# Masking every fourth key block in one call, and issuing the value products a quarter of a block later

## The chip, the core and the metric

The kernel runs on one core of a Trainium2 chip. TensorE (PE) does the matmuls; VectorE (DVE), ScalarE (ACT) and GpSimd (POOL) do the elementwise work; SyncE (SP) issues all DMAs. The metric is the time of one execution on the device in microseconds: the median of three runs is 743.41 us (743.22 to 743.43).

## The reference

One transformer-like block on 2048 tokens of width 512, in float32. A gate mixes sliding-window attention (32 heads of 16 channels, each query sees the 256 keys up to its own) with an MLP that has a tanh GELU:

```python
scores = einsum("bhqd,bhkd->bhqk", q, k) * 16 ** -0.5
mask = (i - j >= 0) & (i - j < 256)
p = softmax(where(mask, scores, -1e9))
a = einsum("bhqk,bhkd->bhqd", p, v) -> (S, 512) @ wo
b = gelu(x @ w1 + b1) @ w2 + b2
g = sigmoid((x * gate_w).sum(-1))
out = g * a + (1 - g) * b
```

## The kernel before

**Two programs woven into one order.** The kernel writes the order of every engine by hand. A *dense* generator (`dense`) yields PE's large work: the projections `qkv`, the MLP (`mlp`, per chunk of 512 tokens and half of the hidden width an *up stage* of `u` tiles and a *down stage* of `y` tiles), and `final` (the output projection). Each step is a group of three matmuls (`mm3`, L109 to L111: high and low halves of the operands), and stands for 681 ns of the order's own clock. `tick` moves this clock on, and `after(ns, fn)` puts an engine's instruction into the program at a later time of it; `need(key)` brings forward what a step depends on. These numbers set only the order in which instructions are written. On the chip each engine takes its list in order and waits on semaphores.

**Attention** is cut into 8 groups of 4 heads and 16 blocks of 128 keys, so 128 units `u`. The main loop (`for u in range(-LEAD, NU)`) handles unit `u` and, 12 units ahead of it, the row maxima of block `m = u + LEAD`. It goes through four quarters `i`; `ORDER` is "m", "s", "p", "f":

- "m": `att_max` makes one tile `sm` of scores (L522, PSUM, at most 320 columns), and VectorE takes its masked row maximum (L527, a reduction and a short read of the accumulator into `M`). The four `sm` tiles of a block come in the order 1, 0, 3, 2 (`XOR`). I call them the first to the fourth.
- "s": `att_exp` makes a tile `st` of transposed scores of unit `u` (L567), with the maxima subtracted through four extra rows of `qs`; ScalarE takes its exponential into `pt` (L589), which holds both key halves (`hf`) and two head pairs of a block. Behind the last of them GpSimd sets to 0 what the window excludes: `sel`, with L583 for each half of the partitions (`r`) and each end of the window (`e`), the near end in columns 0 to 63, the far end in 256 to 319. Three blocks in four have one call of `sel` for both key halves (four selects of 64 x 256 elements); the fourth has one call for each key half (four selects of 64 x 128 each). The last 12 units (`late`) are masked on VectorE (L577).
- "p": at quarter `PVAT`, one unit late, `att_pvs(u - 1)` does the products of the exponentials with the values for a whole chunk of four blocks (L611, 72 or 96 short matmuls), if `u - 1` is the last block of its chunk. It needs the masks of all blocks that it reads, the chunk's own four and up to two ahead of them. There are 32 such calls, 29 of them at `PVAT`; the last three come elsewhere.
- "f": `fill` takes dense steps worth a quarter of `STEP`.

In the up stage a quarter is "m", "s", "p" and one dense step. In the other stages two quarters are joined: "m", "s", "p" of both, and then the dense steps of both.

**What ties them.** `sm` and `st` are PSUM tags of three buffers each, and a call of `att_pvs` takes one of each for its results:

```python
p = ps.tile([128, 320], F32, tag="sm", bufs=3, ...)                  # att_max
p = ps.tile([128, 320], F32, tag="st", bufs=3, ...)                  # att_exp
pv = [ps.tile([128, T], F32, tag=tag, bufs=3, ...) for tag in ("st", "sm")]  # att_pvs
```

A tile gets the buffer that was given back first. So the results of the products get the buffer of the tile three places back in the same tag, and PE waits until VectorE has taken its maximum, or ScalarE its exponential. They go out through ScalarE (L632) and VectorE (L635) into `nd`.

**Other work on the same engines.** Each `u` tile of the MLP passes through ScalarE and VectorE in six steps (`gelu`, L722 to L740). The weights are split into two halves on ScalarE and VectorE (L179, L183). After every fourth block `att_rows` turns the maxima into rows: three short operations on VectorE (L539, L540, L542) and eight copies on GpSimd (L549).

## Time and profile before

| what | before |
|---|---|
| median of three runs | 743.41 us |
| the profiled execution, its span | 745.76 us, 744.0 us |
| ScalarE busy | 57% of the span |
| DMA queue of SyncE | 179168 packets, 170.97 MB, 82.9% of 16 engines |
| chain that ended last | PE 86%, DVE 4%, DMA 4%, ACT 3%, issue 2% |
| PE clock granted | full in all 40 slices |

A row of the timeline gives the start and the duration in us, then engine, line and operation, what is written and read, the sizes, how many instructions are merged and, in brackets, how long the engine stood idle before and what ended that. A row of groups ends with busy time, the mean in ns, and the idle time before them with what ended it. A row of stretches gives the length and then the busy time of PE, weight loads, DVE, ACT and POOL, the granted clock, the share of DMA and GB/s. A matmul's duration contains its passage through the array, so matmuls that follow each other overlap.

### The profile page before, as it was taken

Reading aid. Unit: us, or ns where it says so; the run is one execution under the profiler, and the core shown is the slowest. Engines: PE = TensorE matmul, PEld = TensorE weight load, DVE = VectorE, ACT = ScalarE, POOL = GpSimd, SP = SyncE. Lnnn points to the kernel's source line nnn. Section 1 sums busy time; section 2 is a strip of 40 time slices with the busy share of each in tenths; the row PEclk is TensorE's granted clock in tenths of the full one; section 3 lists DMA queues with packets and bytes.
Section 4 is the critical chain, followed back from the end, with each engine's and each line's share of the span. In section 5 each row is a group of like instructions: output and inputs, shape, how many; then the busy total and the mean of one; then the engine's idle time right before and its main releaser. Section 6 shows DMA issues by size and latency. Waiting matters only on the chain.

```text
span 744.0 us, 17964 instructions
## 1 busy us (share of the span) xinstructions
PE 731.7 (98%) x6129; PEld 604.6 (81%) x6129; DVE 513.6 (69%) x1567; ACT 421.0 (57%) x972; POOL 356.9 (48%) x846
## 2 busy tenths in 40 slices
PE   9999999999999999999999999999999999999998
PEld 7888888887788888888887877888888888878776
DVE  3632325799768867886898789767867886784552
ACT  4434532359447845764695478447735853785450
POOL 4200000349655855776576557746765775620000
PEclk9999999999999999999999999999999999999999
DMA  9989798999994797799567888996799899567573
GB/s 306 351 269 407 262 390 273 267 317 222 262 250 120 176 253 203 172 225 273 148 160 181 223 211 227 252 249 157 178 265 241 177 240 244 137 206 216 175 259 111
DMA packets 179259, 172.12 MB, mean 231 GB/s; under 512 B 56672, under 2 KB 122976, under 8 KB 179168
## 3 DMA queue, kind: packets, MB, share of 16 engines
q1 hardware_dynamic: 179168, 170.97, 82.9%
q8 instruction: 49, 0.80, 0.5%
q14 instruction: 42, 0.34, 0.2%
HBM read 108.53 MB, written 62.39 MB: 230 GB/s over the span
## 4 chain that ended last, share of the span: by engine, by line
PE 86%; DVE 4%; DMA 4%; ACT 3%; issue 2%; SPq 1%; DVEq 0%; ACTq 0%
PE sm L522 9%; PE st L567 8%; PE pv_sm L611 7%; PE y L109 7%; PE y L110 7%; PE y L111 7%; PE u L109 6%; PE u L110 5%; PE u L111 5%; PE qk L109 4%; PE qk L111 4%; PE qk L110 4%; PE v L109 2%; PE v L111 2%; PE v L110 2%; PE pv_st L611 2%
## 5 line engine op out<-in xcount | busy, mean ns | idle before, releaser
L527 DVE CUSTOM_DVE_ANT_0 jm<-sm,mask 128x320 bf16<-128x320 f32 (+4 forms) x512 | 238.1, 465 | 95.6 <-PE sm L522 61.8
L589 ACT ACTIVATE pt<-st 128x320 f32<-128x320 f32 (+4 forms) x512 | 199.2, 424 | 136.5 <-PE st L567 134.5
L583 POOL TENSOR_SCALAR_AFFINE_SELECT pt<-pt 64x256 f32<-64x256 f32 (+1 forms) x538 | 215.3, 420 | 119.0 <-ACT pt L589 108.6
L522 PE MATMUL sm<-kd,qd 96*128 96x320 f32 (+4 forms) x512 | 153.3, 311 | 3.6 <-DVE M L527 3.0
L567 PE MATMUL st<-qs,ks 128*128 128x320 f32 (+4 forms) x512 | 153.8, 309 | 1.1 <-ACT pt L589 1.0
L549 POOL CAST qs<-tt 4x256 fp32r<-4x256 f32 x256 | 120.3, 470 | 55.1 <-DVE tt L542 44.6
L522 PEld LDWEIGHTS sm<-kd,qd 96*128 96x128 f32 x512 | 96.4, 188 | 28.4 <-DVE M L527 8.8
L567 PEld LDWEIGHTS st<-qs,ks 128*128 128x128 f32 x512 | 97.1, 190 | 18.0 <-ACT pt L589 2.4
L109 PE MATMUL y<-w,h 128*128 128x512 f32 x224 | 88.6, 396 | 0.6 <-DVE sqh L728 0.6
L110 PE MATMUL y<-w,h 128*128 128x512 f32 x224 | 88.0, 393 | 0.0
L111 PE MATMUL y<-w,h 128*128 128x512 f32 x224 | 87.9, 393 | 0.0
L109 PE MATMUL u<-mx,w 128*128 128x512 f32 x196 | 80.1, 409 | 0.4 <-DVE sqh L728 0.4
L110 PE MATMUL u<-mx,w 128*128 128x512 f32 x196 | 77.4, 395 | 0.0
L111 PE MATMUL u<-mx,w 128*128 128x512 f32 x196 | 77.1, 393 | 0.0
L611 PE MATMUL pv_sm<-pt,vbuf 64*32 64x320 f32 (+4 forms) x1408 | 73.0, 346 | 0.0
L611 PE MATMUL pv_st<-pt,vbuf 64*32 64x320 f32 (+4 forms) x1408 | 72.7, 346 | 0.0
L611 PEld LDWEIGHTS pv_sm<-pt,vbuf 64*32 64x32 f32 x1408 | 49.4, 106 | 20.2 <-issue 2.4
L326 DVE TENSOR_TENSOR qke<-qk,qke 128x512 fp32r<-128x512 f32 x32 | 22.0, 688 | 46.2 <-ACT qke L323 30.2
L323 ACT ACTIVATE qke<-qk 128x512 fp32r<-128x512 f32 x32 | 19.1, 598 | 56.5 <-PE qk L111 32.9
L111 PEld LDWEIGHTS y<-w,h 128*128 128x128 f32 x224 | 42.1, 188 | 9.8
L109 PEld LDWEIGHTS y<-w,h 128*128 128x128 f32 x224 | 42.4, 189 | 4.6 <-DVE sqh L728 0.8
L339 POOL MEMSET vx<- 128x32 f32 x16 | 2.4, 155 | 89.4 <-DMA SK<-qke 26.6
(148 smaller groups left out, 1329.8 us busy)
## 6 DMA issues: line engine op xcount, KB each, us to landing
kd<-SK SPq DMA_DIRECT2D x32, 384.0 KB
qs<-SQ SPq DMA_DIRECT2D x64, 192.0 KB
mx<-XT SPq DMA_DIRECT2D x24, 512.0 KB
SQ<-qke SPq DMA_DIRECT2D x16, 512.0 KB
SK<-qke SPq DMA_DIRECT2D x16, 512.0 KB
ND<-nd SPq DMA_DIRECT2D x32, 256.0 KB
raw_w<-in_B_w_dram SPq DMA_DIRECT2D x28, 256.0 KB
ks<-SK SPq DMA_DIRECT2D x32, 192.0 KB
```

The source lines that it names most:

```text
L109: nc.tensor.matmul(p, lh, rh, start=first, stop=False)
L110: nc.tensor.matmul(p, lh, rl, start=False, stop=False)
L111: nc.tensor.matmul(p, ll, rh, start=False, stop=last)
L323: nc.scalar.activation(e[:, h], p, AF.Copy)
L326: nc.vector.tensor_sub(e[:, 1 - h], p, f32(e[:, h]))
L522: nc.tensor.matmul(p[:, :w], qd[0:96, n, pr, 128 * j:128 * (j + 1)], kd[0:96, n, pr, k1 - w:k1], start=True, stop=True)
L527: nc.vector.tensor_tensor_reduce(junk[:, :w], p[:, :w], mask[:, 320 - w:320], 1.0, -3e38, ALU.add, ALU.max, M[:, 2 * (b % RB) + hb, pr:pr ...
L549: nc.gpsimd.tensor_copy(dst, src.unsqueeze(1).broadcast_to([4, 2, RB, 32]))
L567: nc.tensor.matmul(p[:, :w], ks[:, slot(g_, kb // NB), pr, at:at + 128], qs[:, pr, k0:k0 + w], start=True, stop=True)
L583: nc.gpsimd.affine_select(out=v, in_=v, pattern=[[0, v.shape[1]], [1 - 2 * e, 64]], compare_op=ALU.is_ge, fill=0.0, base=-e, channel_multi ...
L589: nc.scalar.activation(pt[:, hf, pr, :w], p[:, :w], AF.Exp, scale=SCALE)
L611: nc.tensor.matmul(pv[r // 64][32 * i:32 * i + 32, q - c * T:e - c * T], vts[g_, b // NB][r:r + 64, v:v + 32], rhs(r), start=start, stop=s ...
```

## The change

Two numbers change. `both` no longer leaves out the last block of a chunk, so all blocks that are masked on GpSimd have one call of `sel` for both key halves, behind the last exponential. `PVAT` is 3 in place of 2.

```diff
-        both = not late and kb % NB < NB - 1
+        both = not late
-PVAT = 2
+PVAT = 3
```

On PE, at the products of the last chunk of the first head group, in an up stage (`u_2` is a dense tile, `sm_12_k` and `st_0_k` are tiles k of block 12 and of block 0 of the next head group; `sm_12_1` and `sm_12_0`, the first two of block 12, stand ahead of these rows). Before:

```order
L109 MATMUL u_2_2810<-mx_2149,w_2_1418 128x512
L110 MATMUL u_2_2810<-mx_2149,w_2_1418 128x512
L111 MATMUL u_2_2810<-mx_2149,w_2_1418 128x512
L522 MATMUL sm_12_3_2862<-kd,qd 128x320
L567 MATMUL st_0_2_2865<-qs,ks 128x320
L611 MATMUL pv_3_sm<-pt_10_2471,vbuf 32x64
```

and now:

```order
L109 MATMUL u_2_2796<-mx_2145,w_2_1418 128x512
L110 MATMUL u_2_2796<-mx_2145,w_2_1418 128x512
L111 MATMUL u_2_2796<-mx_2145,w_2_1418 128x512
L522 MATMUL sm_12_3_2848<-kd,qd 128x320
L567 MATMUL st_0_2_2851<-qs,ks 128x320
L109 MATMUL u_2_2796<-mx_2145,w_2_1418 128x512
L110 MATMUL u_2_2796<-mx_2145,w_2_1418 128x512
L111 MATMUL u_2_2796<-mx_2145,w_2_1418 128x512
L522 MATMUL sm_12_2_2862<-kd,qd 128x320
L567 MATMUL st_0_3_2865<-qs,ks 128x320
L611 MATMUL pv_3_sm<-pt_10_2463,vbuf 32x64
```

A dense step, the fourth `sm` tile and the fourth `st` tile now stand ahead of the products. Three places back in `sm` was the first tile of the block (`sm_12_1`), and now is the second (`sm_12_0`). At 13 of the 29 calls five matmuls pass the products in this way; at the other 16, in a down stage, the pair alone does, as here (`sm` of block 4 of the last head group, `st` of block 8 of the one before it), before:

```order
L522 MATMUL sm_4_0_9076<-kd,qd 128x320
L567 MATMUL st_8_1_9080<-qs,ks 128x320
L109 MATMUL y_10_9022<-w_10_6421,h_10_8764 128x512
L110 MATMUL y_10_9022<-w_10_6421,h_10_8764 128x512
L111 MATMUL y_10_9022<-w_10_6421,h_10_8764 128x512
L522 MATMUL sm_4_3_9096<-kd,qd 128x320
L567 MATMUL st_8_2_9099<-qs,ks 128x320
L611 MATMUL pv_1_sm<-pt_2_8664,vbuf 32x64
```

and now:

```order
L522 MATMUL sm_4_0_8984<-kd,qd 128x320
L567 MATMUL st_8_1_8988<-qs,ks 128x320
L109 MATMUL y_10_8934<-w_10_6365,h_10_8674 128x512
L110 MATMUL y_10_8934<-w_10_6365,h_10_8674 128x512
L111 MATMUL y_10_8934<-w_10_6365,h_10_8674 128x512
L522 MATMUL sm_4_3_9004<-kd,qd 128x320
L567 MATMUL st_8_2_9007<-qs,ks 128x320
L522 MATMUL sm_4_2_9010<-kd,qd 128x320
L567 MATMUL st_8_3_9014<-qs,ks 128x320
L611 MATMUL pv_1_sm<-pt_2_8578,vbuf 32x64
```

On VectorE, at the first of these two places (`jm_12_k` is the maximum of `sm_12_k`, the row after it the read of the accumulator). Before:

```order
L527 ISA jm_12_1_2829,M_12_2826<-sm_12_1_2827,mask 128x320
L734 SCALAR_TENSOR_TENSOR x1h_0_2754_2762<-sqh_0_2754_2763,x1h_0_2754_2762 128x512
L728 SCALAR_TENSOR_TENSOR sqh_1_2809_2817<-u_1_2755,x1h_1_2809_2816 128x512
L539 TENSOR_SCALAR nm<-M_8_2565 128x8x2
L540 SCALAR_TENSOR_TENSOR nm<-M_8_2565,nm 128x8x2
L542 STREAM_TRANSPOSE tt<-nm 128x256
L527 ISA jm_12_0_2853,M_12_2826<-sm_12_0_2851,mask 128x320
L527 ISA jm_12_3_2864,M_12_2826<-sm_12_3_2862,mask 128x320
L740 TENSOR_TENSOR h_0_2754<-x1h_0_2754_2762,h_0_2754 128x512
L734 SCALAR_TENSOR_TENSOR x1h_1_2809_2816<-sqh_1_2809_2817,x1h_1_2809_2816 128x512
L635 TENSOR_TENSOR nd_3_2927<-nd_3_2927,pv_3_sm 128x512
L527 ISA jm_12_2_2935,M_12_2826<-sm_12_2_2933,mask 128x320
```

The rows down to the third maximum (`jm_12_3`) are the same now; the fourth, `jm_12_2`, has moved up to directly behind the first L740, ahead of L734 and L635. On GpSimd, around the products of the first chunk (`pt_k` is block k, `xN` the count of equal instructions), before:

```order
L583 AFFINE_SELECT pt_2_1910<-pt_2_1910 64x4x64 x4
L583 AFFINE_SELECT pt_3_1965<-pt_3_1965 64x2x64 x8
L549 CAST qs<-tt 4x2x4x32 x6
L583 AFFINE_SELECT pt_4_2016<-pt_4_2016 64x4x64 x4
L549 CAST qs<-tt 4x2x4x32 x2
```

and now:

```order
L583 AFFINE_SELECT pt_2_1910<-pt_2_1910 64x4x64 x4
L583 AFFINE_SELECT pt_3_1965<-pt_3_1965 64x4x64 x4
L549 CAST qs<-tt 4x2x4x32 x3
L583 AFFINE_SELECT pt_4_2012<-pt_4_2012 64x4x64 x4
L549 CAST qs<-tt 4x2x4x32 x5
```

Block 3 has four selects of twice the width in place of eight, and of the row copies between its masks and those of block 4 three instead of six are left. SyncE issues the same DMAs; the stores of `nd` and what hangs on them move by one or two places.

## The prediction, on record before the changed kernel ran

> **What bounds the kernel now.** I read the page first (busy time by engine), then the busy time by stretch, then who waited for whom on TensorE (PE), and last the timeline around the products of the values, which the change moves.

> ```profile
> PE 731.7 (98%) x6129; PEld 604.6 (81%) x6129; DVE 513.6 (69%) x1567; ACT 421.0 (57%) x972; POOL 356.9 (48%) x846
> 165.00:650.00 485.00, 479.88 (x4618) 398.26 (x4618) 380.39 (x1252) 305.33 (x709) 321.97 (x767) 1.00 0.85 210
> PE sm L522 <- DVE M L527: 3.0, 7, 0.8
> ```

> PE is busy for 731.7 of 744.0 us. In the stretch from 165 to 650 us, where 28 of the 32 calls of `att_pvs` stand (I call such a call a product group; the 29th and last that is moved starts at 650.5), it is busy for 479.88 of 485 us at the full clock. So PE's own work bounds the kernel, and a change gains only what PE waits (about 5 us in that stretch) and loses whatever wait it adds. The change adds no matmul and takes none away. GpSimd (POOL), whose work the change halves in part, is busy for less than half of the span, and in the list of PE's waits no GpSimd instruction stands for this stretch. The longest entry is the third row: PE waits for a row maximum of VectorE (DVE) before a matmul at L522, 3.0 us in 7 times. That kind of wait is the one to follow.

> **Masks.** Of the 128 blocks, 116 are masked on GpSimd, 29 of them in two calls before and in one now.

> ```profile
> L583 POOL TENSOR_SCALAR_AFFINE_SELECT pt<-pt 64x256 f32<-64x256 f32 x334 | 149.1, 467 | 89.7 <-ACT pt L589 84.2
> ...
> L583 POOL TENSOR_SCALAR_AFFINE_SELECT pt<-pt 64x128 f32<-64x128 f32 x204 | 66.1, 343 | 29.3 <-ACT pt L589 24.4
> ...
> L734 DVE SCALAR_TENSOR_TENSOR x1h<-sqh,x1h 128x512 f32<-128x512 f32 x56 | 41.9, 748 | 1.2 <-ACT sqh L731 1.2
> ...
> L728 DVE SCALAR_TENSOR_TENSOR sqh<-u,x1h 128x512 f32<-128x512 f32 x56 | 38.3, 684 | 2.8 <-ACT u L725 2.4
> ```

> The 204 short selects (66.1 us busy, 343 ns mean) become 102 of the long form, at 467 ns 47.6 us: GpSimd loses 18.5 us of work. None of it stands on PE's path, so I cost it at nothing; what hides it is GpSimd's idle time (119.0 us before these selects). The price is at the end of a block: after the last exponential four selects of 467 ns (1.87 us) must run where four of 343 ns (1.37 us) did, so the masks are ready 0.5 us later. The nearest place is this one:

> ```profile
> 327.91 1.27 POOL L583 TENSOR_SCALAR_AFFINE_SELECT pt<-pt 64x128 f32<-64x128 f32 x4 [1.23 <-ACT pt L589]
> ```

> The group that reads these masks starts at 328.90 and will be ready at 329.20 (next part). Its first matmuls need the selects at columns 0 to 64 of both row halves, the first and third of four: 327.91 + 3 x 0.467 = 329.31, a wait of 0.1 us; by all four at their mean 329.78, of 0.6. I take 0.1 and keep 0 to 0.6. At the other groups the last exponential ends at least half a microsecond earlier against the group.

> Two VectorE operations of one size differ by 64 ns, 748 for L734 with both operands in SBUF and 684 for L728 with one in PSUM, over 56 of them 3.6 us, while GpSimd runs beside them. If that loss goes with the count of GpSimd's instructions (102 fewer of 846, 12%), the change gives VectorE 0.4 us back in the whole kernel. [...]

> **Products a quarter later.** In the up stage the group is put behind one more group of three matmuls and one more pair of L522 and L567, in the down stage behind one more pair; the rows stand in the section on the change. The matmuls are the same ones, so their time is nothing by itself. What changes is which buffers the group gets. `sm` has three buffers; a group takes one, and starts only when VectorE has read the tile three places back. Before that is the first of the four `sm` tiles of the block in hand, now the second. For `st` and the exponentials likewise. VectorE does the four maxima in order, and the instructions ahead of the second maximum are the same before and now. So its end can be read from this trace and held against the time at which PE will be ready. In the up stage:

> ```profile
> 228.30 0.31 PE L567 MATMUL st<-qs,ks 128*128 128x320 f32 x1
> ...
> 229.29 0.31 PE L567 MATMUL st<-qs,ks 128*128 128x320 f32 x1
> 229.53 0.24 PE L611 MATMUL pv_sm<-pt,vbuf 64*32 64x64 f32 x1
> ```
> ```profile
> 230.36 0.45 DVE L527 CUSTOM_DVE_ANT_0 jm<-sm,mask 128x320 bf16<-128x320 f32 x1
> 230.75 0.08 DVE L527 DVE_READ_ACCUMULATOR2_ANT M<- 128x1 f32 x1
> ```

> A quarter lasts 229.29 - 228.30 = 0.99 us, so PE will be ready at 229.53 + 0.99 = 230.52. The second maximum, which stands behind the three operations of `att_rows`, ends at 230.83, and PE starts 0.05 us after such an end (379.85 + 0.08 to 379.98, below): a wait of **0.36**. Before, this buffer was wanted only after the group, whose 2 us hid the maximum. In the down stage:

> ```profile
> 599.02 0.31 PE L522 MATMUL sm<-kd,qd 96*128 96x320 f32 x1
> 599.17 0.32 PE L567 MATMUL st<-qs,ks 128*128 128x320 f32 x1
> 599.32 0.32 PE L522 MATMUL sm<-kd,qd 96*128 96x320 f32 x1
> ...
> 600.70 0.24 PE L611 MATMUL pv_sm<-pt,vbuf 64*32 64x64 f32 x1
> ```
> ```profile
> 600.86 0.48 DVE L527 CUSTOM_DVE_ANT_0 jm<-sm,mask 128x320 bf16<-128x320 f32 x1
> 601.27 0.08 DVE L527 DVE_READ_ACCUMULATOR2_ANT M<- 128x1 f32 x1
> ```

> A pair lasts 0.30 us, PE will be ready at 601.00, the maximum ends at 601.35: a wait of **0.40**. The group that waits already before:

> ```profile
> 378.76 0.35 PE L567 MATMUL st<-qs,ks 128*128 128x320 f32 x1
> 379.67 0.30 PE L611 MATMUL pv_st<-nil,vbuf 64*32 64x64 f32 x2 [0.55 <-ACT pt L589]
> 379.98 0.24 PE L611 MATMUL pv_sm<-nil,vbuf 64*32 64x64 f32 x1
> ```
> ```profile
> 379.85 0.08 DVE L527 DVE_READ_ACCUMULATOR2_ANT M<- 128x1 f32 x1
> ...
> 381.41 0.08 DVE L527 DVE_READ_ACCUMULATOR2_ANT M<- 128x1 f32 x1
> ```

> It waits 0.62 us for an exponential (379.67 against 379.05, 0.29 after the matmul before it) and 0.31 for the first maximum, 0.93 together. Now the fourth `sm` tile stands ahead, ready at 378.76 + 0.85 = 379.61 and started at 379.98 (0.37), and the group, ready 0.39 later at 380.37, starts after the second maximum at 381.54 (1.17): 1.54 in all, **0.61** more than before. Two others in the up stage:

> ```profile
> 178.92 0.24 PE L611 MATMUL pv_st<-nil,vbuf 64*32 64x64 f32 x1
> ...
> 180.40 0.08 DVE L527 DVE_READ_ACCUMULATOR2_ANT M<- 128x1 f32 x1
> ...
> 449.33 0.24 PE L611 MATMUL pv_st<-nil,vbuf 64*32 64x64 f32 x1
> ...
> 450.81 0.08 DVE L527 DVE_READ_ACCUMULATOR2_ANT M<- 128x1 f32 x1
> ```

> 178.92 + 0.99 = 179.91 against 180.53, **0.62**; 449.33 + 0.99 = 450.32 against 450.94, **0.62**. Three more groups (328.90, 430.69, 584.96) come close; each costs between nothing and the 0.36 above, and I take 0.1 each, 0.3. At the remaining 21 the second maximum ends before PE is ready.

> Part of this is paid back where VectorE's backlog makes PE wait soon afterwards anyway:

> ```profile
> 186.97 0.42 PE L522 MATMUL sm<-kd,qd 96*128 96x320 f32 x1 [0.79 <-DVE M L527]
> ...
> 464.05 0.41 PE L522 MATMUL sm<-kd,qd 96*128 96x320 f32 x1 [0.36 <-DVE M L527]
> ```

> The first of these follows the group at 178.92 by 8 us, the second ends a row of waits after 449.33. VectorE uses the time that PE stands, so I give back half of the one 0.62 and all of the other. After the groups at 229, 379 and 600 no such wait stands within 10 us, so nothing comes back.

> The sum: 0.36 + 0.40 + 0.61 + 0.62 + 0.62 + 0.3 + 0.1 (masks) = 3.0 us, less 0.3 and 0.6, and less 0.3 for what the new order takes off elsewhere (VectorE can do the fourth maximum while the group runs; an estimate between nothing and the 0.55 of the one exponential wait above): **1.8 us more**. On the queues of SyncE and GpSimd the stores of the group's result and the copies of the rows move with it; nothing on PE waits for these within a block, and I cost them at nothing, with half a microsecond either way. The profiled execution took 745.76 us with a span of 744.0; the median is 743.41. The sum is a difference, so it goes on the median: 743.41 + 1.8 = **745.2 us**.

> **The rivals.** *All is paid back.* VectorE's backlog is a debt that PE pays once, at the group or later; then only the three groups with no later wait count and half of these, and the time is 743.41 + 0.7 = 744.1. For it speaks that 3.0 us of PE's waits hang on the same maxima; against it that three of the five large terms have no wait behind them. *Not slower:* a lighter GpSimd lets VectorE go faster; it decides if the second maximum comes 0.4 to 0.6 us earlier at the five places. Then the added waits fall away and the old 0.93 and some 0.2 elsewhere go: 742.3. Against it stands that the count above gives 0.4 us in the whole kernel. [...] *The masks come last:* if selects wait behind the row copies or run at their mean, a third of the 21 groups that read the newest block's mask first lose some 0.3 us each, 2 us more than forecast: 747.2. Against it, the order on GpSimd keeps these selects ahead of the copies. *The change does not bite,* since the group was waiting for something else anyway: 743.4, against which stands that of PE's waits in this trace one alone, the 0.55 us at 379.67, is of a group for a buffer.

> **How the numbers follow.** About 0.2%, 1.5 us, is what a measurement of this kernel can tell from no change, so slower begins at 744.9. Chances: the forecast 0.52, paid back 0.24 (with no bite), not slower 0.13, masks 0.11. Of the forecast four fifths lie above 744.9, with the masks 0.53 slower; the not-slower case reaches below 741.9 in a third, 0.04 faster; the rest 0.43 is within. The range from 742.8 to 747.0 leaves out the ends of the last two cases.

> **What will show it.** In the changed kernel's waits of PE, L611 behind M of L527 should appear with some 2.5 to 3.5 us, at groups near 180, 231, 381, 451 and 601 us, and the exponential wait at 379 should be gone. L583 should be 436 instructions of one kind, GpSimd some 18 us less busy. Wrong would be: no new wait at L611 (the ring is not what I take it for), or L611 behind POOL pt (the masks), or waits at L522 smaller by as much as L611's are larger (paid back).

## The result, and the profile after

The changed kernel takes 751.84 us (median of six executions, 748.49 to 754.69), the kernel before 743.80 in the same comparison; the ratio is 1.0094 (95% interval 1.0074 to 1.0114). That is 7.0 us more by the ratio, where 1.8 were forecast, and above the range. The profiled execution took 753.69 us, with a span of 751.5.

The page of after (busy time by engine, GpSimd's selects, and the DMA queue that brings PE its instructions):

```profile
PE 735.2 (98%) x6129; PEld 607.7 (81%) x6129; DVE 516.7 (69%) x1567; ACT 422.1 (56%) x972; POOL 335.2 (45%) x744
q8 instruction: 48, 0.79, 0.5%
L583 POOL TENSOR_SCALAR_AFFINE_SELECT pt<-pt 64x256 f32<-64x256 f32 x436 | 196.2, 470 | 150.2 <-ACT pt L589 142.5
```

The selects are as forecast: 436 of one kind at 470 ns, and GpSimd works 21.7 us less (some 18 were forecast). The waits of PE in after (who waited for whom, total, times, longest):

```profile
PE pv_sm L611 <- DVE M L527: 3.2, 6, 1.0
PE sm L522 <- DVE M L527: 2.8, 5, 0.9
PE a L109 <- DVE ao L882: 2.3, 2, 2.1
...
PE y L109 <- issue: 0.8, 1, 0.8
```

The first row is the new wait that was forecast, at its forecast size (2.5 to 3.5 us), and the wait for an exponential at 379 us is gone, as forecast. The timeline of PE in after, cut to the starts of the five groups:

```profile
181.38 0.24 PE L611 MATMUL pv_sm<-nil,vbuf 64*32 64x64 f32 x1 [0.62 <-DVE M L527]
232.65 0.30 PE L611 MATMUL pv_sm<-pt,vbuf 64*32 64x64 f32 x2 [0.39 <-DVE M L527]
384.67 0.24 PE L611 MATMUL pv_sm<-nil,vbuf 64*32 64x64 f32 x1 [1.05 <-DVE M L527]
454.97 0.24 PE L611 MATMUL pv_sm<-nil,vbuf 64*32 64x64 f32 x1 [0.55 <-DVE M L527]
605.24 0.30 PE L611 MATMUL pv_sm<-pt,vbuf 64*32 64x64 f32 x2 [0.38 <-DVE M L527]
```

0.62, 0.39, 1.05, 0.55 and 0.38 us stand against 0.62, 0.36, 1.17, 0.62 and 0.40 worked out beforehand. Two other rows of the waits were not forecast: PE standing for `ao`, a tile of the output that VectorE writes, in the last 35 us (2.3 us, before 1.0), and a stop that nothing in the profile ends ("issue").

How much each place costs shows in **PE's lag**: the dense matmuls (L109 to L111) come in the same order in all these kernels, so the start of the k-th one can be held against the kernel before. From the traces, in us later than before (negative: earlier), by where the matmul stands in the trace of before; the four columns on the right are kernels of the next section:

| at (us, before) | after | e3_last2 | g4_e3_again | f1_tail | g2_free |
|---|---|---|---|---|---|
| 14 | 0.43 | -0.06 | 0.28 | 0.64 | 0.41 |
| 167 | 0.68 | -0.01 | 1.04 | 0.69 | 0.92 |
| 209 | 1.67 | 0.96 | 2.00 | 0.67 | 1.74 |
| 375 | 2.86 | 2.08 | 3.12 | 0.69 | 1.89 |
| 409 | 3.65 | 2.85 | 3.86 | 0.69 | 2.33 |
| 527 | 2.70 | 1.34 | 2.34 | -0.20 | 0.57 |
| 541 | 3.64 | 1.35 | 4.50 | -0.20 | 1.15 |
| 640 | 4.42 | 2.07 | 5.26 | -0.20 | 1.19 |
| 702 | 4.56 | 2.30 | 5.46 | -0.71 | 1.41 |
| 735 | 7.48 | 1.17 | 4.34 | 1.79 | 0.30 |

In after, 0.43 us are the start, which differs between any two executions; 0.94 come at 541 us in one step, 2.9 behind 702. What is left, some 3.2, grows and shrinks around the groups. So the mechanism of the forecast is there, and two others are beside it. The kernel of e3_last2 and g4_e3_again is one and the same, and their two traces lie 1.0 us apart at 209 us and 3.2 at 702: so much can differ between executions.

### The profile page after: what moved, and what is told of

Same layout as the page of the kernel before. It is cut to its first block, busy times and chain, and to the rows that moved or that the text cites. A ratio compares the mean times of both kernels' runs of the same rounds, so it can differ in the third digit from the quotient of the medians.

```text
span 751.5 us, 17862 instructions
## 1 busy us (share of the span) xinstructions
PE 735.2 (98%) x6129; PEld 607.7 (81%) x6129; DVE 516.7 (69%) x1567; ACT 422.1 (56%) x972; POOL 335.2 (45%) x744
## 4 chain that ended last, share of the span: by engine, by line
PE 82%; DVE 6%; DMA 6%; issue 3%; ACT 1%; SPq 1%; POOL 0%; DVEq 0%; ACTq 0%; POOLq 0%
PE sm L522 9%; PE st L567 8%; PE pv_sm L611 7%; PE y L109 6%; PE y L110 6%; PE y L111 6%; PE u L109 6%; PE u L110 5%; PE u L111 5%; PE qk L109 4%; PE qk L111 4%; PE qk L110 4%; DVE jm L527 2%; DMA ND<-nd 2%; PE v L109 2%
## 5 line engine op out<-in xcount | busy, mean ns | idle before, releaser
L527 DVE CUSTOM_DVE_ANT_0 jm<-sm,mask 128x320 bf16<-128x320 f32 (+4 forms) x512 | 238.1, 465 | 75.9 <-PE sm L522 38.5
L589 ACT ACTIVATE pt<-st 128x320 f32<-128x320 f32 (+4 forms) x512 | 197.4, 425 | 138.6 <-PE st L567 136.4
L583 POOL TENSOR_SCALAR_AFFINE_SELECT pt<-pt 64x256 f32<-64x256 f32 x436 | 196.2, 470 | 150.2 <-ACT pt L589 142.5
L567 PE MATMUL st<-qs,ks 128*128 128x320 f32 (+4 forms) x512 | 153.8, 309 | 0.8 <-ACT pt L589 0.8
L522 PE MATMUL sm<-kd,qd 96*128 96x320 f32 (+4 forms) x512 | 151.5, 308 | 3.1 <-DVE M L527 2.8
L549 POOL CAST qs<-tt 4x256 fp32r<-4x256 f32 x256 | 117.8, 460 | 49.3 <-DVE tt L542 38.3
L522 PEld LDWEIGHTS sm<-kd,qd 96*128 96x128 f32 x512 | 96.4, 188 | 24.4 <-DVE M L527 7.6
L567 PEld LDWEIGHTS st<-qs,ks 128*128 128x128 f32 x512 | 97.1, 190 | 18.0 <-ACT pt L589 2.0
L109 PE MATMUL y<-w,h 128*128 128x512 f32 x224 | 90.2, 403 | 1.4 <-issue 0.8
L111 PE MATMUL y<-w,h 128*128 128x512 f32 x224 | 87.8, 392 | 0.0
L109 PE MATMUL u<-mx,w 128*128 128x512 f32 x196 | 80.1, 409 | 0.3 <-DVE sqh L728 0.3
L111 PE MATMUL u<-mx,w 128*128 128x512 f32 x196 | 77.1, 393 | 0.0
L611 PE MATMUL pv_sm<-pt,vbuf 64*32 64x320 f32 (+4 forms) x1408 | 73.3, 346 | 0.9 <-DVE M L527 0.8
L611 PE MATMUL pv_st<-pt,vbuf 64*32 64x320 f32 (+4 forms) x1408 | 72.7, 346 | 0.0
L611 PEld LDWEIGHTS pv_sm<-pt,vbuf 64*32 64x32 f32 x1408 | 50.3, 106 | 20.8 <-issue 3.2
L111 PEld LDWEIGHTS y<-w,h 128*128 128x128 f32 x224 | 42.1, 188 | 9.9
L109 PEld LDWEIGHTS y<-w,h 128*128 128x128 f32 x224 | 42.3, 189 | 7.4 <-issue 2.8
L635 DVE TENSOR_TENSOR nd<-nd,pv_sm 128x512 f32<-128x512 f32 x32 | 21.9, 686 | 37.1 <-ACT nd L632 37.1
```

The costliest lines, as they stand in the source:

```text
L109: nc.tensor.matmul(p, lh, rh, start=first, stop=False)
L111: nc.tensor.matmul(p, ll, rh, start=False, stop=last)
L522: nc.tensor.matmul(p[:, :w], qd[0:96, n, pr, 128 * j:128 * (j + 1)], kd[0:96, n, pr, k1 - w:k1], start=True, stop=True)
L527: nc.vector.tensor_tensor_reduce(junk[:, :w], p[:, :w], mask[:, 320 - w:320], 1.0, -3e38, ALU.add, ALU.max, M[:, 2 * (b % RB) + hb, pr:pr ...
L549: nc.gpsimd.tensor_copy(dst, src.unsqueeze(1).broadcast_to([4, 2, RB, 32]))
L567: nc.tensor.matmul(p[:, :w], ks[:, slot(g_, kb // NB), pr, at:at + 128], qs[:, pr, k0:k0 + w], start=True, stop=True)
```

## The experiments

Beside each the kernel before ran on the same chip; a ratio is to that, with its 95% interval. A trace is of one execution, and the other times of a kernel are of further ones.

**The two edits apart.** `e1_pvat`: `PVAT` alone. `e2_mask`: `both` alone.

> PVAT = 3 alone, the masks in two halves as before. Theory A, all of the loss is the moved products: as the changed kernel, 750 to 752 us (ratio 1.008 to 1.010), with about 3.2 us of PE's waits at L611 behind M of L527. Theory B, the masks that come later are a part of it: 747 us or less, since then the fourth block's masks are half a microsecond earlier than in the changed kernel.

> The masks of every fourth block in one call, PVAT = 2. Theory A, all of the loss is the moved products: 743.4 to 744.2 us (ratio 0.999 to 1.001), no wait at L611 behind M of L527. Theory B, the masks have a part in it: 745 us or more, with waits of L611 behind pt of GpSimd.

750.90 us, ratio 1.0086 (1.0061 to 1.0112), and 746.14 us, 1.0015 (1.0004 to 1.0027). The moved products make most of the loss. The masks alone cost about 1.1 us (0.3 to 2.0), which by ratio lies between the two theories; no wait of L611 for GpSimd stands among PE's waits of e2_mask, and its trace lags by 0.4 us from the start on and by 0.2 more at the end, so where they cost this was not found.

Beside the moved products the traces do show what the masks do. L611 behind M is 2.4 us in e1_pvat, not the 3.2 of the first theory: the five waits are 0.38, 0.29, 0.82, 0.35 and 0.32, together 2.16 where after has 2.99. f4_old_masks, below, which has the masks of before too, has the same five within 0.01, and the six traces that move these groups with the masks in one call and `att_rows` in its place have 3.1 to 3.4 us in that row. The reason stands ahead of the second maximum on VectorE: two of the three operations of `att_rows` take longer. The groups of instructions by line, before and after:

```profile
L539 DVE TENSOR_SCALAR nm<-M 128x16 fp32r<-128x16 f32 x32 | 5.8, 182 | 0.0
L540 DVE SCALAR_TENSOR_TENSOR nm<-M,nm 128x16 fp32r<-128x16 f32 x32 | 5.8, 181 | 1.1
```
```profile
L539 DVE TENSOR_SCALAR nm<-M 128x16 fp32r<-128x16 f32 x32 | 6.8, 214 | 0.0
L540 DVE SCALAR_TENSOR_TENSOR nm<-M,nm 128x16 fp32r<-128x16 f32 x32 | 6.5, 204 | 1.1
```

They are at 187 and 181 ns in e1_pvat and at 213 and 195 in e2_mask, so this goes with the masks. `att_rows` is issued in every fourth unit of the main loop, the one whose masks were changed; near 180 us the four long selects run from 178.1 to 180.6 in after, and the two operations beside them take 0.39 and 0.33 us there, 0.27 and 0.21 in e1_pvat. Why they take longer beside the long selects was not tried.

**The last group, and the rows on VectorE.** `e3_last2` is the changed kernel with the last moved group left at quarter 2; `e4_rows` issues `att_rows` later.

```diff
-                if op == "p" and i == PVAT and 1 <= u <= NU - LEAD:
+                if op == "p" and i == (PVAT if u < NU - LEAD else 2) and 1 <= u <= NU - LEAD:
```
```diff
-            after(900, att_rows, gm, bm // RB)
+            after(2600, att_rows, gm, bm // RB)
```

> The changed kernel, but the last of the 29 product groups stays at quarter 2, which puts SyncE's list after 690 us back to nearly the order of before. Theory T, the tail of the changed kernel (a chain of small transfers behind each other on SyncE's queue, and the lower clock after the wait at 718.6) costs 2.9 us of the 8 and follows from that order: 748 to 749 us, and PE's wait for ao of L882 is about 1.0 us. Rival, the tail is late only because the waits ahead of it make everything late, and SyncE's order has no part in it: as the changed kernel, 751 to 752 us, with the wait for ao still above 2 us.

> The changed kernel, but att_rows is issued 1700 ns later on the order's clock, so that on VectorE its three operations no longer stand ahead of the second maximum. Theory A, the added waits for the second maximum make the loss ahead of the tail (3.2 us at L611 and what follows from them): L611 behind M falls below 1.5 us and the time to 747 to 749 us. Rival, these waits are paid back by fewer waits later, and the loss comes from something else: L611 behind M falls but the time stays within 1 us of the changed kernel's 751.8.

e3_last2: median 749.80 (746.93 to 754.50), ratio 1.0085 (1.0060 to 1.0110); its trace is of the 746.93 one. There PE's wait for `ao` is 0.2 us, under what either theory said, and L611 waits as in after:

```profile
PE pv_sm L611 <- DVE M L527: 3.2, 6, 1.0
...
PE a L109 <- DVE ao L882: 0.2, 1, 0.2
```

Its lag at 702 us, 2.30, is the forecast's own sum (1.8) within half a microsecond, with neither of the two other costs. The median lies between the times of the two theories and is not resolved from after's, so it does not decide between them; f1_tail below does. The other five executions took 1.7 to 7.6 us longer than the one that was traced; that is taken up below. e4_rows: 750.62, ratio 1.0078 (1.0053 to 1.0103). L611 behind M fell from 3.2 to 0.6, PE's waits at L522 rose from 2.8 to 3.5, and one of 0.8 for `sqh` at 167 us is new: 1.5 of the 2.6 us came back at other places. Its lag at 702 is 3.62, of which 1.6 is one "issue" step at 541. The time is 1.2 us under after's, which is not resolved and lies between the two theories, nearer to the rival.

**The last group alone.** `f1_tail` is the kernel before with only this one group moved.

> The kernel before with only the last of the 29 product groups moved to quarter 3; all else as before. Theory T, the tail loses because SyncE's list after 690 us changes with this one group (the load of ot stands ahead of the store of OT it waits for, and the last ND store behind both): PE's wait for ao of L882 grows from 0.8 to over 1.8 us and the time is 1.0 to 3.5 us above the kernel before (ratio 1.0015 to 1.005). Rival, the tail of the changed kernel is late only because PE arrives 4.5 us late there: wait and time as before within 0.5 us.

746.86 us, ratio 1.0031 (1.0014 to 1.0048), 2.3 us (1.0 to 3.6) for one group of 29, as the theory said. PE's waits for `ao` in before and in f1_tail, and then the timeline of SyncE's queue in before and in f1_tail:

```profile
PE a L109 <- DVE ao L882: 1.0, 2, 0.8
```
```profile
PE a L109 <- DVE ao L882: 2.5, 2, 2.3
```
```profile
694.68 0.38 SPq L668 DMA_DIRECT2D OT<-num  x1
695.15 0.38 SPq L656 DMA_DIRECT2D RD<-den  x1
699.80 0.32 SPq L706 DMA_DIRECT2D ot<-OT  x1
...
701.55 0.40 SPq L639 DMA_DIRECT2D ND<-nd  x1
...
707.10 0.59 SPq L649 DMA_DIRECT2D den<-ND  x1
```
```profile
694.03 0.38 SPq L668 DMA_DIRECT2D OT<-num  x1
...
699.90 0.32 SPq L706 DMA_DIRECT2D ot<-OT  x1
...
701.65 0.40 SPq L639 DMA_DIRECT2D ND<-nd  x1
...
706.61 0.59 SPq L649 DMA_DIRECT2D den<-ND  x1
```

The list is a chain: a load of `ot` waits until the store of `OT` has landed (about 5 us), behind it the `ND` store of the last group is issued, and `den` waits for that to land. VectorE's reciprocal (L653) waits for `den` and holds `ao` (L882) up behind it, and PE needs the buffer that `ao` reads. VectorE's timeline in before, f1_tail and after:

```profile
709.94 0.35 DVE L653 RECIPROCAL den<-den 128x32 f32<-128x32 f32 x1 [2.66 <-DMA den<-ND]
```
```profile
710.74 0.35 DVE L653 RECIPROCAL den<-den 128x32 f32<-128x32 f32 x1 [4.16 <-DMA den<-ND]
```
```profile
715.80 0.35 DVE L653 RECIPROCAL den<-den 128x32 f32<-128x32 f32 x1 [3.96 <-DMA den<-ND]
```

In e3_last2 it starts at 711.10. So the reciprocal comes 0.80 us later in f1_tail, 5.86 in after and 1.16 in e3_last2, against a PE that lags by -0.71, 4.56 and 2.30. With the last group moved the chain comes 1.3 to 1.5 us later than PE does, and with it in place 1.1 earlier, which takes up the 0.83 us that PE waits there before. The other traces agree: with the last group moved and the wait not filled PE stands 1.1 to 2.7 us there (five traces), with the group at quarter 2 at most 1.0.

Which step of SyncE's list does it is not shown. The list from the `OT` store on is the same in all four kernels; what the moved group changes stands ahead of that, above all the places of two stores (`ND` at 655 us in before, `OT` at 679). In after the `OT` store at 700.34 is already 1.1 us later than PE is; in f1_tail that store is no later than PE, and it is the landings that take longer, 5.9 us from the `OT` store to the load of `ot` where before had 5.1, and 4.1 from the `den` load to the reciprocal where before had 2.8.

**The clock behind the wait.** In after the wait for `ao` is followed by matmuls at twice their distance. The timeline of PE:

```profile
716.10 0.39 PE L111 MATMUL a<-wo,ot 128*128 128x512 f32 x1
718.62 0.50 PE L109 MATMUL a<-wo,ot 128*128 128x512 f32 x1 [2.12 <-DVE ao L882]
718.95 0.40 PE L110 MATMUL a<-wo,ot 128*128 128x512 f32 x1
...
720.86 0.63 PE L110 MATMUL a<-wo,ot 128*128 128x512 f32 x1
721.29 0.63 PE L111 MATMUL a<-wo,ot 128*128 128x512 f32 x1
```

The last two start 0.43 us apart, where 0.23 is usual. The busy time by stretch there (length, PE, weight loads, DVE, ACT, POOL, granted clock, DMA share, GB/s):

```profile
716.20:719.70 3.50, 1.38 (x7) 0.90 (x6) 3.50 (x6) 1.73 (x3) 0.00 (x0) 1.00 0.57 179
719.70:723.10 3.40, 3.40 (x10) 2.63 (x9) 0.12 (x1) 0.00 (x0) 0.00 (x0) 0.50 0.82 236
723.10:726.50 3.40, 3.40 (x17) 2.78 (x15) 1.17 (x2) 1.25 (x2) 0.00 (x0) 1.00 0.98 298
```

Half the clock for 3.4 us costs 1.7 us, beside the 2.1 of the wait itself. `f2_busy` fills the wait of the changed kernel with nine matmuls.

```diff
+                    if (t, b, e) == (1, 2, 0):
+                        fp = ps.tile([128, T], F32, tag="sm", bufs=3, name="fp")
+                        for _ in range(9):
+                            nc.tensor.matmul(fp, ot[e][:, 0, ts], w[:, 0, cs], start=True, stop=True)
```

> The changed kernel with nine extra matmuls (2.1 us of PE's work whose result nobody reads) put ahead of the matmul that waits for ao of L882 near 718 us. Theory C, the lower clock that follows this wait comes from PE standing idle: no matmul at 427 ns distance after it, the clock 1.0 in the stretch from 720 to 740 us in every run that has no other wait of that length, and the median 0.7 to 1.7 us below the changed kernel's. Rival, the clock falls there for another reason: half-rate matmuls remain, and the time stays.

750.82 us, ratio 1.0089 (1.0069 to 1.0109). Five of six executions have a mean clock of 1.0 and one 0.999, where four of six of the changed kernel have 0.995 to 0.999; the traced one has 1.00 from 720 to 740 and no matmul at half rate. So the drop goes with PE standing idle, but not every stand brings it: behind the waits of 2.32 us in f1_tail and 2.71 in e4_rows the clock stayed at 1.00. The time was not resolved: the lag grows by 2.5 us there where it was 2.9, since the nine take the wait's place.

**PE's own instructions.** The stop in after that nothing ends, in the timeline of PE:

```profile
543.49 0.31 PE L567 MATMUL st<-qs,ks 128*128 128x320 f32 x1
544.60 0.39 PE L109 MATMUL y<-w,h 128*128 128x512 f32 x1 [0.80 <-issue]
```

The row of queue 8 in the result says that PE's 12,482 instructions (6129 matmuls, as many weight loads and 224 others) come in 48 packets, 0.79 MB, so 16 KB and 260 instructions each. The traces give the start and the duration of every packet. Eight times PE stops around the landing of one and starts again 1.2 to 1.7 us behind it:

| execution | packet lands (us) | PE starts again | PE stood |
|---|---|---|---|
| after | 543.1 | 544.60 | 0.80 |
| e4_rows | 542.4 | 544.04 | 1.46 |
| g4_e3_again | 544.0 | 545.43 | 1.99 |
| f2_busy | 544.2 | 545.94 | 1.17 |
| f2_busy | 203.2 | 204.39 | 1.08 |
| e1_pvat | 203.4 | 204.78 | 1.65 |
| g2_free | 202.1 | 203.53 | 0.79 |
| g2_free | 540.5 | 541.97 | 0.29 |

The profile puts the ones at 204.39 and 203.53 down to `yo` of VectorE, which in f2_busy had ended 0.44 us before PE started and whose result that matmul doesn't use. What ends these stops shows in a count: whenever PE stopped it had begun exactly 2241 or 8897 of its instructions (weight loads, matmuls and semaphores in the trace). The two numbers are 26 x 256 apart, and both are 449 more than 256 for each packet that had landed over 1.2 us before. In none of the 17 traces is PE ever further ahead of the packets than that. So PE had used up what had come, at the cut between two packets.

A group of the products takes 192 or 144 of the 256 instructions of a packet within 2 us, and dense work takes 10 in a quarter of 0.99 us, so one group and some 6 to 11 us of dense work use a packet up (an estimate). The one that lands at 543 in after was served at 531.1 in before. `f3_shift` (on e3_last2) and `h_after48` (on the changed kernel) move the cuts between packets by 96 instructions, `g1_cuts` moves them in the kernel before; `f4_old_masks` is e3_last2 with the masks of before.

```diff
+        for _ in range(SMALL if n == WARM[0] else 0):
+            nc.tensor.matmul(p[0:32, 0:32], idle[:, 0:32], idle[:, 0:32], start=True, stop=True)
```

> The kernel with the last group left at quarter 2 (e3_last2), and 48 small matmuls (32 x 32) more at the very start, which shift the places where PE's instruction stream is cut into 16 KB packets by 96 of 256 instructions. Theory F, the late instruction packets (each late one stops PE for about a microsecond, and which are late hangs on where the cuts stand against the transfers) make a part of the loss and of the scatter of 747 to 754.5 us: other packets are late than the 24th, 28th and 33rd, and the median of the times moves by over 1.5 us from 749.8, up or down, more than the start costs (about 1 us). Rival, the cuts have no part in it: the median stays within 1.5 us and the same stretches are slow.

> PVAT = 3 with the masks of before, the last group left at quarter 2. Theory A + T (added waits and tail are separate, the masks do nothing): as e3_last2, 746.9 us in an execution without late instruction packets, 749 to 750 in the median. Rival, the late masks are part of the loss: below 747 in the median, and the lag of PE behind the kernel before at 690 us is under 1.5 us.

f3_shift: 749.59 us (748.61 to 750.22), ratio 1.0071 (1.0055 to 1.0086). No stop without a releaser, and the executions lie within 1.6 us where e3_last2's lay within 7.6 (and within 2.4 when the same program ran again, below); but the median stayed, which is what the rival said. In its trace a wait of VectorE for ScalarE near 161 us costs PE 1.3 us. f4_old_masks: 748.83, ratio 1.0058 (1.0037 to 1.0078), not resolved from e3_last2; its lag at 690 us is 2.45, of which 1.3 is a wait for `sqh` near 440 us that no other trace has at this size.

> e3_last2 once more, since its one trace was of the fastest of its six executions (746.9, median 749.8). Theory F, the slower executions have late instruction packets (the 24th above all, which came within a few instructions of stopping PE) and lowered clock: this trace shows one or more waits of PE without a releaser or a chain that a late transfer began, that account for its time above 746.9. Rival, the slower executions have longer waits for the second maximum: L611 behind M above 4 us.

749.25 us (747.76 to 750.20), ratio 1.0053 (1.0037 to 1.0069). The traced one took 750.12, and the waits of PE answer the question:

```profile
PE pv_sm L611 <- DVE M L527: 3.1, 6, 1.0
PE sm L522 <- DVE M L527: 3.1, 6, 0.9
PE y L109 <- issue: 2.0, 1, 2.0
```

It is the same program as e3_last2 and waits as long for the maxima. Of the 3.2 us between the two traces 2.15 are this one step (table of lags, 527 to 541), the rest stands in front of 210 us. The packet was another than the theory had named, the one before 543 us, not the 24th.

> The kernel before with 104 small matmuls (32 x 32) more at the very start and no other edit, so that the cut of PE's instruction stream that stood ahead of the products near 535 us comes 72 instructions later: the packet is asked for at 532 us instead of 528, inside the burst of transfers, as in the changed kernel. Theory F (a late packet stops PE, and which is late hangs on the cuts): a wait of PE with no releaser of 0.3 to 1.5 us near 541 to 545 us, which no execution of the kernel before has shown; the time 1 to 2.5 us above the kernel before, of which about 0.7 is the start. Rival, the stops come with the moved products themselves: no such wait, and the time under 1 us above.

746.00 us, ratio 1.0015 (1.0002 to 1.0029), and no stop; the start alone lags by 1.6 us. The packet landed at 542.9, as meant, and by the count above PE still had 20 instructions left 1.2 us later.

> The kernel before with 120 small matmuls at the very start in place of g1_cuts' 104, so that the same packet is asked for 32 instructions earlier, 2 us. Theory F: if it still lands near 543 us, 290 instructions start between request and landing, and PE stops for 1 to 1.5 us without a releaser near 542 to 545 us. If it is served before the burst (landing before 537 us), no stop, and the run says nothing. Rival, the stops come with the moved products: no stop though 282 or more instructions lie between.

> The same with 128 small matmuls: the packet is asked for 48 instructions earlier than in g1_cuts. Theory F: landing near 543 us, 300 or more instructions and a stop of 1.5 to 2 us; or served before the burst and no stop. Rival as for h_cuts120.

> The changed kernel with 48 small matmuls at the very start, which moves the cuts as f3_shift does. Theory F: no packet lands 282 or more instructions behind its request, no wait of PE without a releaser above 0.3 us, the tail's wait for ao as in the changed kernel (about 2 us); the ratio to the kernel before falls from 1.0094 to 1.006 to 1.008. Rival, the stop at 541 us belongs to the moved products: it stays, and so does the ratio.

h_cuts120 and h_cuts128 (one execution each, 746.63 and 746.83 us): the packet landed at 539.9 and at 534.2, and neither stopped PE. In the kernel before no stop was brought about; whether one can come without moved products stays open. h_after48: 749.76 us, ratio 1.0066 (1.0045 to 1.0086), as theory F said, against 1.0094 of the changed kernel; no stop without a releaser is among its waits. But its trace does not gain by that: at 702 us it lags by 4.49, as after does (4.56), 0.65 of it from the start, with a wait of 0.57 at 690 us that after lacks. It is faster behind 702, where the wait for `ao` is 1.2 us, not 2, and the clock stays up. So the lower median is not shown to be the price of the stop.

**The waiting groups left alone.** `g2_free` is e3_last2 with eight more groups left at quarter 2, the six at which PE waits in after and two near 436 and 589 us that miss the list of its waits; 20 stay moved.

```diff
-                if op == "p" and i == PVAT and 1 <= u <= NU - LEAD:
+                if op == "p" and i == (2 if u in EARLY else PVAT) and 1 <= u <= NU - LEAD:
+EARLY = [4 * n + 4 for n in (0, 3, 8, 12, 15, 16, 24, 25, 28)]
```

> The kernel with the last group left at quarter 2 (e3_last2), with eight more groups left at quarter 2: those at which the changed kernel waits for the second maximum (near 180, 233, 316, 383, 436, 454, 589 and 605 us). 20 of 29 groups stay moved. Theory A, the loss ahead of the tail is these waits: L611 behind M below 0.3 us, PE's lag behind the kernel before at 690 us below 0.8 us where it was 2.3 (late packets apart), and the median 1.5 to 2.5 us below that of e3_last2 run beside it. Rival, moving a group costs in itself: the lag at 690 us stays above 1.5 us without a wait at L611.

746.10 us, ratio 1.0014 (0.9996 to 1.0032), 3.2 us under g4_e3_again beside it. L611 behind M is not among its waits any more, the wait for the exponential at 380 is back (0.6), and the lag at 702 us is 1.41, of which 0.41 is the start and 1.5 are two late packets (near 203 and 541 us), so that without these it would be half a microsecond ahead of before. Moving 20 groups costs nothing that the masks of e2_mask don't.

**A quarter earlier.** `g3_pvat1`: the kernel before with `PVAT = 1`.

> The kernel before with the products a quarter earlier (PVAT = 1), nothing else. Theory A says that the ring is no limit there (the tile three places back is of the block before, long read), so the existing waits at L611 go; but the masks of the newest block then have 1 us less in an up stage and 2 us less in a down stage: waits of L611 behind pt of GpSimd of 0.3 to 1 us at many of the 29 groups, 750 to 765 us. Rival, the masks have room: 742 to 743 us, and quarter 1 is better than 2.

751.51 us, ratio 1.0084 (1.0067 to 1.0101). The waits of PE that are new there:

```profile
PE pv_sm L611 <- POOL pt L583: 1.4, 4, 0.5
...
PE pv_st L611 <- POOL pt L583: 0.8, 2, 0.4
```

The masks do come last there, but in six waits, not at many groups. Quarter 2 is the best of the three; no kernel of this study beats the kernel before.

## Why the prediction was wrong, point by point

- **The ring of `sm`** was right: the wait and its places. L611 behind M is 3.2 us, forecast at 2.5 to 3.5; the 0.2 beside the five places are of a group at 316 us that was not named. That the sizes fit so well is in part luck: 0.8 of the 2.99 us at the five places come from the masks, through slower operations of `att_rows`, where the prediction took the end of the second maximum from the trace of before. With the masks of before the five are 2.16, against 3.17 worked out.
- **The payback** was right as a mechanism at one of its two places. Between 409 and 527 us the lag falls by 0.95 in after and by 1.5 in e3_last2, where 0.6 was forecast; e4_rows shows the same debt from its other side, 1.5 of 2.6 us. The 0.3 to be given back at 187 us was not: that wait grew from 0.79 to 0.92.
- **The sum of these**, 1.8 us, is 2.30 in e3_last2, by lag at 702 us. Leaving out the eight waiting groups brings the median down by 3.2 us (g2_free), late packets included.
- **"On the queues of SyncE and GpSimd the stores ... move with it; ... I cost them at nothing, with half a microsecond either way"**: this is the step that failed. For the 20 groups that g2_free moves it holds; for the last one, whose store stands in a chain of three transfers that waits for each landing, it costs 2.3 us (f1_tail). In after's trace the 2.9 us behind 702 are 1.3 of wait and 1.6 of half the clock, which followed this wait and not every such wait. The sum said that nothing on PE waits for these "within a block", and behind the last group there is no block.
- **The stop for instructions** was no term and no rival. It costs 0.3 to 2.0 us where it comes, once or twice in six of the eight executions traced with 20 or more groups at quarter 3 and the cuts in place, and in none of the two with the cuts moved. It may also be why the changed kernel scatters over 6 us where the kernel before scatters over 3. That it is a late packet is shown by the count of instructions at the stops. How much it adds to the median is not: f3_shift, without stops, had the same median, and h_after48 was faster at another place.
- **The masks** were mis-sized: 0.1 us was taken and 0 to 0.6 kept; e2_mask measured 1.1 (0.3 to 2.0), and with the moved products they lengthen the waits for the second maximum by 0.8. Waits of L611 for GpSimd, the place named, are not it. The prediction also had VectorE gain 0.4 us from fewer GpSimd instructions, an estimate by their count; L734, at 748 ns before, is at 752 ns in after, and L539 and L540 together lost 1.7 us.
- Together by the medians: 1.1 for the masks, about 4 for the eight waiting groups with their packets and the masks' part in their waits (mean of e3_last2's two ratios, 1.0069, against 1.0014), about 2 for the last group; 7.0 measured. The two ratios of e3_last2 differ by 2.4 us, so each part is good to a microsecond or two.
- **Not slower**, **all is paid back** and **the masks come last** did not come about as told. The time of the last, 747.2, is the nearest of them and still 3.2 us short of the 750.4 that the ratio gives, and its mechanism is not among the waits.

## What to carry to other kernels

When a step of a hand-written order is moved, follow what it issues on every queue to the end of the program, the last instance by itself: what the instances before it hide, the last one can pay. A chain of transfers that waits for each landing can have slack against the compute engine (1.1 us in e3_last2) or hold it up (f1_tail, where PE waits 2.5 us for `ao` in place of 1.0). The places at which a ring of buffers will make an engine wait can be read from the trace of before, and the sizes to a few tenths of a microsecond, if the durations stay; here two short operations did not keep theirs (182 to 214 ns, 181 to 204), since the work that GpSimd does beside them had changed. And a kernel whose PE is busy for 98% has costs that no wait of before announces: whether the next packet of instructions comes in time (stops of 0.29 to 1.99 us here).

## What the runs showed of the hardware

```profile
535.00:540.00 5.00, 5.00 (x104) 3.90 (x110) 4.57 (x16) 2.63 (x6) 3.66 (x7) 1.00 0.98 227
540.00:545.00 5.00, 4.20 (x43) 3.46 (x28) 3.02 (x11) 2.13 (x5) 4.52 (x12) 1.00 1.13 257
```

The granted clock fell to 0.50 for 3.4 us behind a wait of 2.12 us in after, and stayed at 1.00 behind one of 2.71 us in e4_rows and one of 2.32 us in f1_tail. So the length of the wait alone does not tell whether the clock falls; what does is not shown.
